# Near and global keys laid out behind each block's own, and attention in steps of eight heads

## The chip, the cores and the metric

One core of a Trainium2 chip runs the whole program. The metric is the device time of one execution in microseconds (us); lower is better. Engines are named as in the profile: PE is TensorE's matmul stream, PEld its weight loads, DVE is VectorE, ACT ScalarE, POOL GpSimd, SP SyncE, whose queue issues nearly all loads.

## The reference, cut to what matters

Attention over 4 batches, 8 heads, 768 positions of 64 features; then a feed-forward layer 512 to 2048 to 512 on 3072 tokens; then a mixture of eight experts with 384 tokens each.

```python
n_global, n_local = (8, 96)
...
is_global = pos[None, :] < int(n_global)
is_local = (rel >= 0) & (rel < int(n_local))
keep = is_global | is_local
dist = np.where(is_global & ~is_local, float(n_local), np.abs(rel).astype(np.float32))
...
scores = scores + bias[None, :, :, :]
scores = np.where(keep, scores, -1000000000.0)
...
a = a / (np.sum(a, axis=-1, keepdims=True) + 1e-09)
return np.matmul(a, v).astype(np.float32)
...
h = x @ w_in
g = h * (1.0 / (1.0 + np.exp(-h)))
return (g @ w_out).astype(np.float32)
```

A block of 128 queries needs its own 128 keys, the 95 keys in front of it and the 8 global ones: 103 keys beside its own.

## The kernel before

**Tiling.** Attention works on 24 blocks of 128 tokens (six per batch). A group is four heads of one block; there are 48 groups. For each group `scores` (L413) issues four matmuls of 64 rows by 256 columns in float32 (128 columns for the first block of a batch, which has nothing in front): two heads at a time lie on the two halves of the array's rows, and their scores go to two PSUM banks taken from the ring `TP` (banks 0, 1, 2). Then, per pair of heads, the softmax: a DVE operation that adds the table of distances and finds the maximum (L453), an exponential on ACT (L457), and on DVE the reciprocal of the sum (L461, L462) and the scaling (L464). `turn` (L468) transposes the probabilities of two pairs on PE (L478) and ACT copies each to SBUF (L482). `weigh` (L485) multiplies them with the values: eight matmuls of 128 columns (L500), into bank 5. After the second group of a block `features` (L505) splits the result in two parts for the feed-forward layer.

The 256 keys are those of the block and of the whole block before it. `keys` (L377) keeps two halves of one tile for each group of heads, the even and the odd block, and loads each block's keys once; from the third block of a batch on, POOL first copies the eight global keys into the half of the block in front (L387). `values` (L401) has three buffers and loads eight global rows into the older one (L408).

**The feed-forward layer** works on chunks of two blocks: sixteen items a chunk, each `item` (L538) being 12 matmuls of 256 columns (L552), a tanh and a few elementwise operations (L566 to L572), and `product` (L575) six matmuls of 512 columns (L587 to L589). The hidden values of items go to the ring `HB` (banks 3 and 4); the accumulators lie in banks 6 and 7.

**Order.** The program is written as slots (L739, L780). Where chunks 2 to 9 are worked on, a slot holds one item and its predecessor's product, and `a` counts the slots by heads: every fourth slot visits a group. In that visit PE does the values of the group four slots back and the scores of the new one as one task (from slot `PAIRED` = 56 on), and two slots later `turn`. A planner then orders all tasks: `Plan.order` (L188) simulates five engines with guessed durations, and of the tasks that are ready it starts the one with the lowest `pri` (by default the order in which they were written). The gate's dot products on DVE (L659) have 200 added to theirs, so they go last. Within an engine the order is then fixed.

Early on (slots up to 55, chunks 0 and 1) attention runs ahead of the feed-forward layer, whose weights are loaded as 8-byte numbers and converted by ACT, DVE and POOL (L354 to L372).

After the front part, `Back` routes tokens and runs the experts; it reuses the attention's buffers (L1512) for its small tables, and gathers and scatters rows with 48 indirect DMAs issued by POOL (L1311, L1430).

Of the kernel before, what the change touches and what calls it, by code (L numbers as in the profile page):

```python
# [225 lines left out]

def sub_ap(ap, offset, dims):
    return bass.AP(tensor=ap.tensor, offset=ap.offset + offset, ap=[list(d) for d in dims])
# [6 lines left out]
class Front:  # L235


    def __init__(self, tc, plan, room, banks, main, small, pages, qT, kT, vT, w_in, w_out, w_gate, n_global, n_local, x2d, L,
                 xd=None, dbg=None):
        self.tc, self.nc, self.p = tc, tc.nc, plan  # L240
        self.room, self.banks, self.main, self.small, self.pages = room, banks, main, small, pages
        self.qT, self.kT, self.vT = qT, kT, vT
# [24 lines left out]
    def consts(self):  # L267
# [4 lines left out]
        t = self.banks.take(6, lambda t: t.rearrange("p a b -> p (a b)"))  # L272
# [6 lines left out]
        p.add(PE, 0.427 * NWARM, warm, r=[one], w=[t])  # L279
# [3 lines left out]
        base = self.once("v20", [128, 4, 128], BF16, self.small)  # L283

        self.T = self.once("T", [128, H, 3, 128], BF16, self.small)
# [3 lines left out]
        def near():  # L289
# [4 lines left out]
            g.affine_select(T[:, 1], t, pattern=[[1, 128]], compare_op=ALU.is_ge, fill=MASK, base=nl - 1,  # L294
# [7 lines left out]
            if ng < 128:  # L302
                nc.vector.tensor_copy(T0[:, ng:], T[:, 1, ng:])

        def before():

            r, T = rel()[:, 0], base()
            g.iota(r, pattern=[[1, 128]], base=-128, channel_multiplier=-1, allow_small_or_imprecise_dtypes=True)
            g.affine_select(T[:, 0], r, pattern=[[1, 128]], compare_op=ALU.is_ge, fill=MASK, base=nl - 129,
                            channel_multiplier=-1)  # L310
            if ng:
                g.memset(T[:, 0, :ng], -float(nl))
            nc.vector.tensor_copy(T[:, 2], T[:, 0])
# [15 lines left out]
        for h in range(H):  # L329
            p.add(DVE, 0.2, lambda h=h: nc.vector.tensor_scalar(part[h](), base()[:, :3], 2.0 ** (2 - h), None, op0=ALU.mult),  # L330
# [46 lines left out]
    def keys(self, bl, e):  # L377

        nc, p, ng = self.nc, self.p, self.ng
        i, j = bl % NB, bl % 2  # L380
        if e not in self.K:
            t = self.once(f"k{e}", [128, 2, 2, 128], F32, self.small)
            self.K[e] = t, t.parts(*(lambda t, j=j: t[:, :, j] for j in range(2)))
        t, b = self.K[e]
# [4 lines left out]
        p.add(SP, 0.6, lambda: nc.sync.dma_start(b[j](), self.half_block(self.kT, bl, e)), w=[b[j]],  # L389
              pri=12 * e + 24 * bl - 99 if bl < DB else None)  # L390

    def half_block(self, t, bl, e):
        return sub_ap(t, bl * 128 * DM + 256 * e, [[DM, 128], [1, 256]]).rearrange("p (a s) -> p a s", a=2)
# [7 lines left out]
    def values(self, bl, e):  # L401
        nc, p, ng = self.nc, self.p, self.ng
        c = 4 * e * D
        rows = lambda n, bl: self.vT[bl * 128:bl * 128 + n, c:c + 4 * D].rearrange("s (h d) -> s h d", d=D)
        if bl % NB > 1 and ng:

            w = self.V[bl - 1, e]
            p.add(SP, 0.6, lambda: nc.sync.dma_start(w()[:ng], rows(ng, bl - bl % NB)), w=[w])  # L408
        v = self.V[bl, e] = self.once(f"v{bl % 3}{e}", [128, 4, D], F32, self.small)
        p.add(SP, 0.6, lambda: nc.sync.dma_start(v(), rows(128, bl)), w=[v], pri=12 * e + 24 * bl - 90 if bl < DB else None)  # L410


    def scores(self, u, before=None):  # L413

        nc, p = self.nc, self.p
        bl, h0 = divmod(u, H)
        i = bl % NB
        n = 1 if i == 0 else 2
        e = h0 // 4
        k, kb = self.K[e]  # L420
        q = self.qs[bl, e]
        s = [self.half("tp", 4) for _ in range(2)]

        def qk():
            for a in range(2):
                for j in range(2):
                    r = slice(64 * j, 64 * j + 64)
                    nc.tensor.matmul(s[j]()[:, n * a:n * a + n], q()[r, a], k()[r, a, :n], start=True, stop=True)  # L428

        if before:  # L430
            dur, av, r, w, then = before

            def both():
                av()
                qk()

            p.add(PE, dur + 0.43 * n, both, r=[*r, q, *kb[:n]], w=[*w, *s])
            then()
        else:
            p.add(PE, 0.43 * n, qk, r=[q, *kb[:n]], w=s)  # L440
        for a in range(2):
            z = self.ring("z", NZ, [128, 2, 2, 128], F32)
# [3 lines left out]
            for j in range(2):  # L446
# [3 lines left out]
                def soft1(a=a, j=j, h=h, nb=nb, zs=zs):  # L450
                    T = self.Th[h]()
                    t = self.T0h[h]()[:, None] if i == 0 else (T[:, 1:3] if i % 2 == 0 else T[:, 0:2])
                    nc.vector.tensor_tensor_reduce(zs[j]()[:, :n], s[j]()[:, n * a:n * a + n], t, -0.125, 3.0e38, ALU.add,  # L453
                                                   ALU.min, nb())

                p.add(DVE, t_dve(128 * n), soft1, r=[s[j], self.T0h[h] if i == 0 else self.Th[h]], w=[zs[j], nb])
                p.add(ACT, 0.1 + 0.2 * n, lambda j=j, nb=nb, zs=zs, ss=ss: nc.scalar.activation(  # L457
                    zs[j]()[:, :n], zs[j]()[:, :n], AF.Exp, bias=nb(), scale=-1.0, accum_out=ss[j]()),
                      r=[nb], w=[zs[j], ss[j]], lat=0.09)
            v = nc.vector  # L460
            p.add(DVE, 0.073, lambda r=r, sm=sm: v.tensor_scalar(r(), sm(), 1e-9, None, op0=ALU.add), r=[sm, *ss], w=[r])  # L461
            p.add(DVE, 0.1, lambda r=r: v.reciprocal(r(), r()), w=[r])  # L462
            for j in range(2):
                p.add(DVE, t_fast(128 * n), lambda j=j, zs=zs, r=r: v.tensor_scalar(  # L464
                    zs[j]()[:, :n], zs[j]()[:, :n], r()[:, j:j + 1], None, op0=ALU.mult), r=[r], w=[zs[j]])
            self.z[u + 2 * a] = zs

    def turn(self, u):  # L468
        nc, p = self.nc, self.p
        n = 1 if (u // H) % NB == 0 else 2  # L470
        for a in range(2):
# [13 lines left out]
    def weigh(self, u):  # L485
# [8 lines left out]
        vs = [self.V[bl - (bl + b) % 2, h0 // 4] for b in range(n)]  # L494
# [285 lines left out]
    def slot(self, a, items, ws):  # L780
# [13 lines left out]
        if near and a is not None and a % 4 == 0:  # L794
            w = self.weigh(a - 4) if unit(4) else None
            if w and not (unit(0) and a >= PAIRED):
                dur, av, r, o, then = w
                self.p.add(PE, dur, av, r=r, w=o)
                then()
                w = None  # L800
            if unit(0):
                self.scores(a, w)
        if near and unit(2) and a % 4 == 2:
# [745 lines left out]
```

## Time and profile before

| | us |
|---|---|
| median of 3 runs | 1089.94 |
| lowest, highest | 1089.39, 1091.43 |
| the profiled execution's own time | 1091.94 |
| its span, first to last instruction | 1090.2 |
| PE busy in the span | 1049.2 (96%) |
| DVE busy | 817.4 (75%) |
| ACT busy | 489.9 (45%) |
| POOL busy | 153.1 (14%) |

The profile is of one execution. Its span leaves out 1.7 us before the first and after the last instruction. A row of the timeline gives start, duration, engine, line, operation, and what is written and read; matmuls are pipelined, so the spacing of starts tells more than durations. "Idle before" is what the engine waited, and for whom. A row of the table by stretches gives the stretch, its length, the busy time and number of instructions of each engine, TensorE's granted clock as a share of full speed, and the DMA engines' share and rate.

### The profile page before, as it was taken

What the parts mean: (1) busy time and instruction counts of PE and PEld (TensorE: products, weight loads), DVE (VectorE), ACT (ScalarE), POOL (GpSimd) and SP (SyncE); (2) the same over time, 40 slices, a digit from 0 to 9 for tenths busy, and PEclk for the clock granted to TensorE, in tenths of its full rate; (3) what the DMA queues carried; (4) which work ended last, traced back from release to release, by engine and by line L of the source; (5) the groups of instructions that cost most, each with busy time, mean ns of one, the idle gap of its engine ahead of it and who ended that gap; (6) DMA issues with size and microseconds to landing.
All of it is one profiled execution on the core that took longest, in us unless ns stands there. A gap on an engine that the chain in (4) does not pass through costs nothing.

```text
span 1090.2 us, 20764 instructions
## 1 busy us (share of the span) xinstructions
PE 1049.2 (96%) x7541; PEld 893.0 (82%) x7541; DVE 817.4 (75%) x2734; ACT 489.9 (45%) x1243; POOL 153.1 (14%) x172
## 2 busy tenths in 40 slices
PE   7879989999999999999999999999999999999997
PEld 4657778888888888888888889976778888888996
DVE  7999768969596969787787866547878888984431
ACT  5766544454444444444444444413343443433431
POOL 2434541101000101000000000000011203211111
PEclk8989999999999999999999999999899999999999
DMA  5555532110111101120101100005336434524510
GB/s 176 159 159 158 170 107 69 31 49 21 45 45 29 36 30 51 31 64 21 45 17 50 31 26 2 1 20 174 108 107 213 132 119 175 174 93 162 176 64 29
DMA packets 71719, 91.79 MB, mean 84 GB/s; under 512 B 5312, under 2 KB 54720, under 8 KB 71616
## 3 DMA queue, kind: packets, MB, share of 16 engines
q1 hardware_dynamic: 67776, 77.87, 22.4%
q0 software_dynamic: 3840, 12.59, 3.4%
q8 instruction: 59, 0.97, 0.4%
q14 instruction: 44, 0.36, 0.1%
HBM read 77.86 MB, written 12.58 MB: 83 GB/s over the span
## 4 chain that ended last, share of the span: by engine, by line
PE 68%; issue 7%; DVE 7%; DMA 2%; POOL 1%; ACT 1%; POOLq 0%; SPq 0%; ACTq 0%; DVEq 0%
PE bank L552 20%; PE bank L1391 9%; PE bank L1417 8%; PE bank L587 7%; PE bank L588 6%; PE bank L589 6%; PE bank L500 3%; PE bank L428 3%; PE bank L478 2%; PE bank L1079 1%; PE bank L1332 1%; PE bank L682 1%; POOL out_dram L1430 1%; DMA st__9177<-in_moe_w_dram 1%; DMA out_dram<-wl__10561,v__8959 1%
## 5 line engine op out<-in xcount | busy, mean ns | idle before, releaser
L387 POOL TENSOR_SCALAR k__84<-k__84 128x16 f32<-128x16 f32 x16 | 4.6, 288 | 176.0 <-PE bank L428 108.7
L387 POOL TENSOR_SCALAR k__120<-k__120 128x16 f32<-128x16 f32 x16 | 4.1, 256 | 139.1 <-PE bank L428 78.7
L1079 PEld LDWEIGHTS <-z__8685 128*128 128x128 bf16 x280 | 9.6, 97 | 8.8 <-issue 3.6
L1311 POOL DMA_INDIRECT wl__9185<-x2d,v__8959 x1 | 1.3, 1336 | 97.9 <-DVE wh__9187 L1373 97.9
L1128 DVE TENSOR_SCALAR_CACHE_REDUCE v__8094<-bank 128x8 f32<-128x8 f32 (+1 forms) x28 | 4.4, 158 | 13.0 <-PE bank L1079 13.0
L634 DVE DVE_READ_ACCUMULATOR2_ANT L<- 128x1 f32 x160 | 12.9, 81 | 0.0
L1079 PEld LDWEIGHTS <-z__8695 128*128 128x128 bf16 x280 | 9.5, 96 | 1.5 <-issue 1.4
L1079 PEld LDWEIGHTS <-z__8690 128*128 128x128 bf16 x280 | 9.5, 96 | 0.0
L1321 PE MATMUL bank<-q__7831 128*128 128x512 bf16 x32 | 9.1, 439 | 0.0
L1372 ACT ACTIVATE wl__9009<-st__8966 128x512 fp32r<-128x512 f32 x1 | 0.6, 632 | 18.5 <-DMA st__8966<-in_moe_w_dram 18.5
L1321 PEld LDWEIGHTS <-q__7831 128*128 128x128 bf16 x32 | 3.1, 106 | 6.1 <-issue 3.9
L1069 DVE TENSOR_TENSOR z__8685<-v__8735,q__7831 128x1024 bf16<-128x1024 f16 (+1 forms) x14 | 7.8, 555 | 0.0
L1069 DVE TENSOR_TENSOR z__8690<-v__8735,q__7831 128x1024 bf16<-128x1024 f16 (+1 forms) x14 | 7.7, 550 | 0.0
L1069 DVE TENSOR_TENSOR z__8695<-v__8735,q__7831 128x1024 bf16<-128x1024 f16 (+1 forms) x14 | 7.7, 550 | 0.0
L1079 PE MATMUL bank<-v__8094,z__8685 128*128 128x8 bf16 x160 | 7.1, 168 | 0.0
L1131 PEld LDWEIGHTS <-q__7831 128*128 128x128 bf16 x28 | 2.7, 98 | 5.3 <-issue 5.0
L1079 PE MATMUL bank<-v__8094,z__8695 128*128 128x8 bf16 x160 | 6.9, 167 | 0.0
L1079 PE MATMUL bank<-v__8094,z__8690 128*128 128x8 bf16 x160 | 6.8, 166 | 0.0
L1430 POOL DMA_INDIRECT out_dram<-wl__11117,v__8959 x1 | 2.7, 2744 | 28.3 <-ACT wl__11117 L1429 28.3
L603 ACT ACTIVATE ax__8789<-bank 128x512 f32<-128x512 f32 x1 | 0.6, 598 | 12.8 <-PE bank L589 12.8
L277 PE MATMUL bank<-jk__77 128*128 128x512 bf16 x10 | 4.4, 631 | 1.5 <-DVE jk__77 L273 1.5
L1069 DVE TENSOR_TENSOR z__8685<-v__8735,q__7664 128x512 bf16<-128x512 f16 (+1 forms) x14 | 5.9, 419 | 0.0
(8066 smaller groups left out, 4579.9 us busy)
## 6 DMA issues: line engine op xcount, KB each, us to landing
k__84<-in_k_dram SPq DMA_DIRECT2D x24, 128.0 KB, 2.2
k__120<-in_k_dram SPq DMA_DIRECT2D x24, 128.0 KB, 2.2
st__189<-in_moe_w_in_dram SPq DMA_DIRECT2D x1, 512.0 KB, 3.9
st__230<-in_moe_w_out_dram SPq DMA_DIRECT2D x1, 512.0 KB
st__273<-in_moe_w_in_dram SPq DMA_DIRECT2D x1, 512.0 KB
st__346<-in_moe_w_out_dram SPq DMA_DIRECT2D x1, 512.0 KB
st__393<-in_moe_w_in_dram SPq DMA_DIRECT2D x1, 512.0 KB, 4.2
st__425<-in_moe_w_out_dram SPq DMA_DIRECT2D x1, 512.0 KB, 4.3
```

The lines of the kernel that those rows point to most:

```text
L428: nc.tensor.matmul(s[j]()[:, n * a:n * a + n], q()[r, a], k()[r, a, :n], start=True, stop=True)
L478: nc.tensor.transpose(pt()[:, n * j + b], zs[j]()[:, b], self.ident())
L500: nc.tensor.matmul(o()[64 * j:64 * j + 64, h0 // 2 + a], vs[b]()[:, 2 * a + j], ps[a]()[:, n * j + b], start=b == 0, stop=b == n - 1)
L552: nc.tensor.matmul(h(), w, x(d), start=k == 0, stop=k == 11)
L587: nc.tensor.matmul(a(), gh()[:, j], oh(), start=f == 0, stop=False)
L588: nc.tensor.matmul(a(), gh()[:, j], ol(), start=False, stop=False)
L589: nc.tensor.matmul(a(), gl()[:, j], oh(), start=False, stop=f == NF - 1)
L1069: self.p.add(DVE, t_fast(n * CPART), lambda s=s, c=c, sh=sh: v.tensor_tensor(c().rearrange("p b (j w) -> p b j w", w=2), key()[:, s, None, ...
L1079: nc.tensor.matmul(cnt(), cs[j](b), D()[:, i], start=i == 0, stop=i == NBLK - 1)
L1391: nc.tensor.matmul(h()[:, :RB], w()[:, d], x(), start=d == 0 and i == 0, stop=d == 3 and i == 2)
L1417: nc.tensor.matmul(a(), g()[:, j], w(), start=f == 0 and i == 0, stop=f == NF2 - 1 and i == 2)
L1430: p.add(POOL, 1.1, lambda: nc.gpsimd.indirect_dma_start(out=self.out[k * RB + j], out_offset=bass.IndirectOffsetOnAxis(ap=self.idx[k]()[:, ...
```

## The change

The host lays out, for each block and head pair, the block's own 128 keys and behind them `W2` = 104 others: 8 global, 95 near, 1 of padding. The values of these 104 come as a second tensor. So `scores` works on 232 columns instead of 256, the tables and the softmax too, `turn` transposes 128 and 104 columns, and `weigh` contracts over 128 and 104 rows. The copy of global keys on POOL and the small loads of global values go; key loads have two buffers per group of heads, and there is a load of far values beside the load of own values. From slot 56 to 183 attention goes in steps of eight heads: `visit` does, as one task on PE, the values of the two older groups and the scores of the two new ones, one of whose four banks is taken from the items' ring (`"h"`); the four pairs are turned two, three, five and six slots later. The second group's softmax has its `pri` raised by `LATE`, a second pair's by `STEP`. The buffers of turned probabilities go from three to four. The ring of POOL's DMA descriptors is halved.

```diff
+        ts = [self.banks.take(i, lambda t: t.rearrange("p a b -> p (a b)")) for i in (*TP0, HB[0])]
...
-                nc.tensor.matmul(t(), one()[:, :128], one(), start=True, stop=True)
+                nc.tensor.matmul(ts[i % len(ts)](), one()[:, :128], one(), start=True, stop=True)
...
-        if i > 1 and ng:
-
-            p.add(POOL, 0.174, lambda: nc.gpsimd.tensor_scalar(b[1 - j]()[:, :, :ng], b[j]()[:, :, :ng], 1.0, 1.0,
-                                                               ALU.mult, ALU.mult), r=[b[j]], w=[b[1 - j]])
...
+        t = self.K[bl, e] = self.once(f"k{e}{bl % 2}", [128, 2, 128 + self.W2], F32, self.small)
+        self.p.add(SP, 0.6, lambda: self.nc.sync.dma_start(t(), self.half_block(self.kT, bl, e)), w=[t],
+                   pri=12 * e + 24 * bl - 99 if bl < DB else None)
...
-            p.add(SP, 0.6, lambda: nc.sync.dma_start(w()[:ng], rows(ng, bl - bl % NB)), w=[w])
...
+        for x, src, n in (("v", self.vT, 128), ("vb", self.vB, self.W2))[:1 if bl % NB == 0 else 2]:
+            v = self.once(f"{x}{bl % 2}{e}", [128, 4, D], F32, self.small)
+            p.add(SP, 0.6, lambda v=v, src=src, n=n: nc.sync.dma_start(
+                v()[:n], src[bl * n:(bl + 1) * n, c:c + 4 * D].rearrange("s (h d) -> s h d", d=D)),
...
+    def visit(self, new, old):
+
+        done = [self.weigh(u) for u in old]
+
+        new = [self.scores(u, len(new) == 2 and i == 0, LATE * i) for i, u in enumerate(new)]
+        todo = [*done, *new]
+
+        def all():
+            for t in todo:
+                t[1]()
+
+        self.p.add(PE, sum(t[0] for t in todo), all, r=[b for t in todo for b in t[2]],
+                   w=list({id(b): b for t in todo for b in t[3]}.values()))
+        for t in todo:
+            t[4]()
...
+        s = [self.half("h" if more and j else "tp", 4) for j in range(2)]
...
+                    self.nc.tensor.matmul(flat(s[j])[:, 256 * a:256 * a + n], q()[r, a], k()[r, a, :n], start=True, stop=True)
...
+        first = len(p.tasks) + late
         for a in range(2):
-            z = self.ring("z", NZ, [128, 2, 2, 128], F32)
+            pri = first + (STEP * a if PAIRED <= u < ALONE else a)
+            z = self.ring("z", NZ, [128, 2, 256], F32)
...
-                        nc.tensor.transpose(pt()[:, n * j + b], zs[j]()[:, b], self.ident())
+                        w = (128, self.W2)[b]
+                        nc.tensor.transpose(pt()[:w, n * j + b], zs[j]()[:, 128 * b:128 * b + w], self.ident())
...
-                        nc.tensor.matmul(o()[64 * j:64 * j + 64, h0 // 2 + a], vs[b]()[:, 2 * a + j], ps[a]()[:, n * j + b],
+                        nc.tensor.matmul(o()[64 * j:64 * j + 64, h0 // 2 + a], vs[b]()[:rows[b], 2 * a + j], ps[a]()[:rows[b], n * j + b],
...
+            if PAIRED <= a < ALONE:
+                if r == 0:
+                    self.visit([a + 4, a], [a - 4] if a == PAIRED else [a - 8, a - 4])
+                if r in TURNS:
+                    self.turn(a - r + TURNS[r][0], [TURNS[r][1]])
...
-NZ, NP = 4, 3
-PAIRED = 56
+NZ, NP = 4, 4
+
+PAIRED, ALONE, LATE, STEP = 56, NU - H, 40, 20
+TURNS = {2: (4, 0), 3: (4, 1), 5: (0, 0), 6: (0, 1)}
...
-    nc = bacc.Bacc("TRN2", target_bir_lowering=False, num_devices=1, dynamic_dma_scratch_size=8192)
+    nc = bacc.Bacc("TRN2", target_bir_lowering=False, num_devices=1, dynamic_dma_scratch_size=4096)
```

## Rows read from the trace of the kernel before

**Rows 1.** Busy time, share of the span and instructions, whole run: TensorE.
```profile
PE 1049.2 (96%) x7541; PEld 893.0 (82%) x7541; DVE 817.4 (75%) x2734; ACT 489.9 (45%) x1243; POOL 153.1 (14%) x172
```

**Rows 2.** Busy time by stretches: two early ones, and the stage of chunks 2 to 9.
```profile
0.00:54.50 54.50, 44.45 (x270) 30.51 (x270) 47.01 (x166) 35.59 (x100) 18.10 (x31) 0.87 0.55 167
54.50:109.00 54.50, 45.16 (x294) 35.34 (x295) 49.65 (x121) 35.59 (x87) 23.68 (x22) 0.94 0.53 158
...
163.50:654.00 490.50, 488.44 (x3485) 423.02 (x3485) 396.15 (x1400) 227.40 (x657) 30.31 (x45) 1.00 0.12 38
```

**Rows 3.** Waits of PE between 163 and 654 us, longest first: line, releaser, us.
```profile
PE bank L478 <- DVE z__6587 L464: 0.8, 1, 0.8
```

**Rows 4.** Timeline of PE: a visit with 256 keys, one with 128.
```profile
452.66 0.39 PE L589 MATMUL bank<-wh__1348,gl__5473 128*128 128x512 f32 x1
452.98 0.44 PE L500 MATMUL bank<-ph__5458,v__4854 128*64 128x128 f32 x4
...
454.00 1.13 PE L428 MATMUL bank<-k__120,q__5011 64*128 64x256 f32 x8
455.06 0.50 PE L587 MATMUL bank<-wh__1460,gh__5499 128*128 128x512 f32 x1
455.40 0.39 PE L588 MATMUL bank<-wl__1469,gh__5499 128*128 128x512 f32 x1
...
511.75 0.44 PE L500 MATMUL bank<-ph__6162,v__5563 128*64 128x128 f32 x4
...
512.34 0.72 PE L428 MATMUL bank<-k__120,q__5723 64*128 64x128 f32 x8
512.98 0.38 PE L552 MATMUL bank<-xTh__5000,wh__1588 128*128 128x256 f32 x1
```

**Rows 5.** Scores, timeline of L428: slots 64 and 176, 28 groups apart.
```profile
L428 PE MATMUL bank<-k__84,q__1803 x8: 376/376/480, 211.1 to 211.9; 64*128 64x256 f32 x8
...
L428 PE MATMUL bank<-k__84,q__6961 x8: 376/376/480, 614.0 to 614.8; 64*128 64x256 f32 x8
```

**Rows 6.** Timeline of PE: one pair turned, and the matmul behind it.
```profile
447.80 0.60 PE L478 MATMUL bank<-ident__79,z__5375 128*128 128x128 f32 x4
448.15 0.48 PE L587 MATMUL bank<-wh__1219,gh__5422 128*128 128x512 f32 x1
```

**Rows 7.** Weight loads of scores (64 rows) and items (128 rows), ns min/median/max.
```profile
L428 PEld LDWEIGHTS bank<-k__84,q__4847 x8: 182/186/187, 440.9 to 441.5; 64*128 64x128 f32 x8
...
L552 PEld LDWEIGHTS bank<-xUh__4287,wh__1185 x4: 186/192/192, 442.0 to 443.1; 128*128 128x128 f32 x4
```

**Rows 8.** Timeline of DVE: softmax at 256 and at 128 columns, a gate dot.
```profile
443.55 0.41 DVE L453 CUSTOM_DVE_ANT_0 z__5375<-bank,T__141 128x256 f32<-128x256 f32 x1
...
443.89 0.42 DVE L453 CUSTOM_DVE_ANT_0 z__5393<-bank,T__141 128x256 f32<-128x256 f32 x1
...
446.32 0.61 DVE L464 TENSOR_SCALAR z__5375<-z__5375,r__5417 128x256 f32<-128x256 f32 x2
...
7.15 0.29 DVE L453 CUSTOM_DVE_ANT_0 z__159<-bank,T__122 128x128 f32<-128x128 f32 x1 [1.32 <-PE bank L428]
...
7.37 0.29 DVE L453 CUSTOM_DVE_ANT_0 z__159<-bank,T__122 128x128 f32<-128x128 f32 x1
...
8.80 0.48 DVE L464 TENSOR_SCALAR z__159<-z__159,r__181 128x128 f32<-128x128 f32 x2
...
440.52 0.69 DVE L659 CUSTOM_DVE_ANT_0 jk__5351<-xl__5235,st__1783 128x512 bf16<-128x512 f32 x1
```

**Rows 9.** Copies of global keys on POOL (L387) in the first stretch.
```profile
0.00:54.50 54.50, 1.87 (x6) 0.87 0.55 167
```

**Rows 10.** Timeline of the start: first load of keys, first scores.
```profile
0.80 0.44 SPq L389 DMA_DIRECT2D k__84<-in_k_dram  x1
...
5.89 1.23 PE L428 MATMUL bank<-k__84,q__113 64*128 64x128 f32 x8
```

**Rows 11.** Timeline of POOL: the last scatter, with POOL's idle time before.
```profile
1084.46 0.97 POOL L1430 DMA_INDIRECT out_dram<-wl__13194,v__8959  x1 [1.07 <-ACT wl__13194 L1429]
```

More of the change, by code (lines that the diff above doesn't have):

```diff
@@ L401, in values, with scores @@
     def values(self, bl, e):
-        nc, p, ng = self.nc, self.p, self.ng
+        nc, p = self.nc, self.p
         c = 4 * e * D
-        rows = lambda n, bl: self.vT[bl * 128:bl * 128 + n, c:c + 4 * D].rearrange("s (h d) -> s h d", d=D)
-        if bl % NB > 1 and ng:
-            w = self.V[bl - 1, e]
-            p.add(SP, 0.6, lambda: nc.sync.dma_start(w()[:ng], rows(ng, bl - bl % NB)), w=[w])
[L409 to L415, printed above, removed]
+        self.V[bl, e] = []
+        for x, src, n in (("v", self.vT, 128), ("vb", self.vB, self.W2))[:1 if bl % NB == 0 else 2]:
+            v = self.once(f"{x}{bl % 2}{e}", [128, 4, D], F32, self.small)
+            p.add(SP, 0.6, lambda v=v, src=src, n=n: nc.sync.dma_start(
+                v()[:n], src[bl * n:(bl + 1) * n, c:c + 4 * D].rearrange("s (h d) -> s h d", d=D)),
+                  w=[v], pri=12 * e + 24 * bl - 90 if bl < DB else None)
+            self.V[bl, e].append(v)
+    def visit(self, new, old):
[9 more added lines that the diff above has]
+            t[4]()
+    def scores(self, u, more=False, late=0):
         bl, h0 = divmod(u, H)
-        i = bl % NB
-        n = 1 if i == 0 else 2
         e = h0 // 4
-        k, kb = self.K[e]
-        q = self.qs[bl, e]
-        s = [self.half("tp", 4) for _ in range(2)]
+        n = 128 if bl % NB == 0 else 128 + self.W2
+        k, q = self.K[bl, e], self.qs[bl, e]
+        s = [self.half("h" if more and j else "tp", 4) for j in range(2)]
         def qk():
@@ L427, in qk, with softmax @@
                     r = slice(64 * j, 64 * j + 64)
[L428 to L440, printed above, removed]
+                    self.nc.tensor.matmul(flat(s[j])[:, 256 * a:256 * a + n], q()[r, a], k()[r, a, :n], start=True, stop=True)
+        return 0.43 * n / 128, qk, [q, k], s, lambda: self.softmax(u, s, late)
+    def softmax(self, u, s, late):
+        nc, p = self.nc, self.p
+        bl, h0 = divmod(u, H)
+        i = bl % NB
+        n = 128 if i == 0 else 128 + self.W2
+        first = len(p.tasks) + late
         for a in range(2):
-            z = self.ring("z", NZ, [128, 2, 2, 128], F32)
+            pri = first + (STEP * a if PAIRED <= u < ALONE else a)
+            z = self.ring("z", NZ, [128, 2, 256], F32)
             zs = z.parts(*(lambda t, j=j: t[:, j] for j in range(2)))
@@ L493, in weigh @@
         ps = [self.P.pop(u + 2 * a) for a in range(2)]
-        vs = [self.V[bl - (bl + b) % 2, h0 // 4] for b in range(n)]
+        vs = self.V[bl, h0 // 4]
+        rows = 128, self.W2
         def av():
@@ L792, in slot @@
             self.weights(u)
[L794 to L803, printed above, removed]
-            self.turn(a - 2)
+        if near and a is not None and a >= 0:
+            r = a % 8
+            if PAIRED <= a < ALONE:
[3 more added lines that the diff above has]
+                    self.turn(a - r + TURNS[r][0], [TURNS[r][1]])
+            else:
+                if r % 4 == 0:
+                    old = [u for u in ((a - 8, a - 4) if a == ALONE else (a - 4,)) if 0 <= u < NU]
+                    if a < PAIRED and old:
+                        self.visit([], old)
+                        old = []
+                    if old or unit(0):
+                        self.visit([a] if unit(0) else [], old)
+                if r % 4 == 2 and unit(2):
+                    self.turn(a - 2)
         for c, f in items:
@@ L1494, in attention_moe_kernel @@
         x2d = dp.tile([NTOK, DM], F32, name="x2d")
[L1496 removed]
+        near = is_near(n_global, n_local)
         xd = None
```

100 lines of the change are left out of this document (56 added, 44 removed).

## Prediction

> **What bounds the kernel now.** First the page's busy times: PE is busy for 96% of the span [rows 1]. That is an average, so next the busy times by stretches [rows 2]. From 163.5 to 654 us, where chunks 2 to 9 and most of attention run, PE is busy for 488.4 of 490.5 us at the full granted clock (1.00), while DVE has 396.2, ACT 227.4 and POOL 30.3. In the first 109 us it is otherwise: PE is busy for 44.5 and 45.2 of 54.5 us, DVE for 47.0 and 49.7. The view of waits says whether PE's busy time hides stalls: in the long stage its longest wait is 0.8 us, for a softmax's scaling [rows 3]. So in that stage only work that leaves PE counts, and early on work that leaves DVE counts most. What attention costs PE is read from the timeline. From the scores of slot 64 to those of slot 176 are 402.9 us, or 14.4 us for a group and its four items [rows 5].
>
> One visit [rows 4]: the last matmul of an item starts at 452.66, and the next of its kind would start 0.23 later (the usual spacing, 0.23 us); the values start at 452.98, 0.09 late. Values to scores is 1.02, scores to the next item 1.06, and that item's first matmul takes 0.34 to the second, 0.11 more than usual. Together 2.28 us. A visit in a block with nothing in front has half the values and half the columns: 0.59 and 0.64 [rows 4]. The differences, 0.43 and 0.42, are the price of the work itself; so 0.16 us (1.02 less twice 0.43) and 0.22 us (1.06 less twice 0.42) are spent whatever the amount. With 0.09 and 0.11 a visit has **0.58 us of fixed cost** and 1.70 us of work.
>
> **The change, part by part.**
>
> *Two visits become one.* From slot 56 to slot 184 there are 33 visits before and 17 after (56, 64 and so on to 184), each with all values first and all scores behind. 16 visits go. If the second group's matmuls follow the first's without a break, each takes its 0.58 us along: 16 x 0.58 = 9.3 us. If the part of the scores is paid for each group anyway, 0.36 is left and 5.8 us. I take 9.3: inside one visit four pairs of matmuls already follow each other at the price of the work, and a second group is more of the same.
>
> *232 columns for 256 in the scores.* 0.42 us for 128 columns [rows 4] is 3.3 ns a column, 79 ns a group for 24 columns. From slot 56 on there are 34 groups, four of them in first blocks of a batch: 30 x 0.079 = 2.4 us, all on PE. The bounds are nothing (if weight loads, 186 ns [rows 7], keep the spacing up) and 2.4; I take 2.4.
>
> *Values over 104 rows, turns of 104 columns.* The values' matmuls stream 128 columns of probabilities as before, over fewer rows. The rows show no price for rows: a weight load with 64 rows takes 186 ns, one with 128 rows 186 to 192 [rows 7]. The Trainium skill says the same of the loads in "TensorE: Matmul & The Clock Gate", section "LDWEIGHTS (loading the stationary operand)": their time goes with the columns and not with the contraction dimension. By that rule, which speaks against much of what this change cuts, this part is worth nothing; priced by rows of keys it would be what the second rival below has. I take nothing for the values. A turn of a pair is 0.35 us from its start to the next item's [rows 6]; half of it has 104 columns of weights instead of 128, but the same 128 columns stream, so I take nothing here and keep 30 x 2 x 0.35 x 0.5 x 24/128 = 2.0 us as the upper bound. There are four turns for eight heads before and after.
>
> *Softmax.* The maximum takes 0.34 us at 256 columns and 0.22 at 128, start to start [rows 8]: 0.9 ns a column; two scalings 0.61 and 0.48, 1 ns a column of both. A group (four maxima, two pairs of scalings) saves 24 x (4 x 0.9 + 2 x 1.0) = 0.13 us on DVE. In the long stage PE covers it (DVE has 94 us free there [rows 2]); if that cover goes it would be 30 x 0.13 = 4 us. Early there are ten groups with 256 keys: 1.3 us, which counts where DVE is the bound.
>
> *Copies of global keys.* Six copies, 1.87 us of POOL in the first 54.5 us [rows 9], and with them the wait of a key load for the copy, behind which SP's weight loads stand. I take 0.7 us for that. So the early stage gives 2 us. It is also where the order may shift: bounds -3 and +5 us, a few of the 20 us for which PE idles there [rows 2].
>
> *Loads.* By their shapes, the keys of a group go from 128 to 232 KB, and 40 loads of 104 KB stand where 32 loads of 8 KB stood: 8.9 MB more, some 2.5 MB of it before 163 us, and eight more issues on SP at about 0.44 us [rows 10]. The DMA engines are 0.55 and 0.53 busy early and 0.12 later [rows 2], so this goes beside other work. A key load now has two buffers and waits only for the scores two blocks back. The first load is issued at 0.80 and the first scores start at 5.89, behind the warm-up matmuls [rows 10]; a load nearly twice as long fits in that. If the cover went, 2.5 MB at 160 GB/s [rows 2] would be 16 us; that is a rival.
>
> *What waits.* The one PE task for eight heads waits for four turned pairs and four banks at once, and the next item's matmuls stand behind it on PE. The last pair is turned two slots ahead (5.6 us); its copy on ACT is ready long before. The scores of slot a+4 come four slots earlier, with their whole softmax; the older group's values come four slots later, which is what the fourth buffer is for. The items' ring lends a bank: below.
>
> *The end.* A smaller descriptor ring could make POOL wait. Its last scatter came after 1.07 us of idle time [rows 11] and POOL is busy for 14% [rows 1]; nothing, upper bound about 1 us on the last scatter.
>
> Sum: 9.3 + 2.4 + 2 = 13.7 us. The profiled execution took 1091.94 us; 1078.2 after. It is 2.0 us above the median of 1089.94, so the median forecast is 1076.2, say **1076 us**. What is late next is still PE, in the same stage.
>
> **The rivals.**
>
> *The fixed cost stays with the group* (chance 0.12). If the 0.58 us belong to each group's change of shapes rather than to the visit, only columns and the early stage pay: 2.4 + 2 = 4.4 us, 1085.5. For it: values and scores each have their own share. Against it: within a visit nothing is paid between pairs.
>
> *Everything shrinks by the keys* (0.07). If values and turns also cost by keys, a group saves another 0.43 x 24/128 + 0.066 = 0.15 us, 30 times 4.4 us: 1071.6. Against it stand the weight loads [rows 7].
>
> *The borrowed bank stalls PE: slower* (0.07). Each eight-head visit takes one of the items' two banks, so the second item behind it cannot start until DVE has read four sets of scores from that visit. PE has the other scores (about 0.8), an item and a product (14.4 - 2.28 - 0.86, over four, is 2.8) to do meanwhile: 3.7 us. DVE needs 4 x 0.34 = 1.4 us and may have a feature split and an item's two operations in front (1024 columns at 0.9 ns and three times some 0.1 us of start, as the maxima [rows 8] have it: 1.3 us), as well as gate dots of 0.69 us [rows 8]. With one dot it holds by 0.3 us. It decides when the stall passes 13.7 / 16 = 0.86 us a step, that is from two more dots in front; then it is 1.1 us, 17.6 in all, 3.9 us slower: 1093.8. Against it: dots have the lowest priority. The Trainium skill, in "TensorEngine Tiling (Array Packing)", section "Gotcha 1: PSUM Pressure", warns of this side of row tiling: different row tiles write to different banks, so eight heads side by side ask for four. By that rule alone the time would be this rival's; the kernel before takes two banks a visit and hardly waits [rows 3], so no row here shows the case of four.
>
> *The early loads give it back: no change* (0.05). If the larger loads were not hidden, up to 16 us early against 13.7: about 1090.
>
> **How the numbers follow.** The forecast has 0.69. Its own bounds: 5.8 to 9.3 for the visits, 0 to 2.4 for columns, 0 to 2 for turns, -3 to +5 early; taken together mostly 8 to 17 us, 1073 to 1082. The range goes on to the second rival and over the first, 1070 to 1086, and leaves out the other two and some of the early stage. About 0.2% (2.2 us) is what a measurement can tell from no change. Faster by more: 0.69 + 0.12 + 0.07 = 0.88; slower: 0.06 of the 0.07; the rest, 0.06, within.
>
> **What would show it.** In the changed profile a full visit should last 2 x 1.70 + 0.58 - 0.16 = 3.8 us where two took 4.6; eight heads with eight items 28.0 us instead of 28.8; PE without waits in the stage; the copies gone. It is wrong if PE waits in that stage for DVE in front of an item, if a visit lasts over 4.3 us, or if the stage begins later than before by more than 3 us.

## The result, and the profile after

The changed kernel takes 1081.49 us (median of 6 runs, 1078.96 to 1084.85), the kernel before, run beside it, 1090.12. The ratio is 0.9913 with an interval of 0.9891 to 0.9935: 9.5 us less (7.1 to 11.9); the two medians themselves are 8.6 us apart. The forecast was 1076, with a range of 1070 to 1086; it was on the right side, 5.5 us too low. One run of the kernel before, of 1659 us, lies far above its other five and is left out of the ratio. The profiled execution took 1079.03 us, with a span of 1077.3.

The page's line of busy times of the changed kernel answers to [rows 1]:

```profile
PE 1033.2 (96%) x7541; PEld 893.0 (83%) x7541; DVE 809.1 (75%) x2733; ACT 487.0 (45%) x1243; POOL 143.8 (13%) x141
```

TensorE has as many instructions as before and is busy for 16 us less, at the same 96%. POOL has 31 instructions fewer: the copies are gone. To see where the time went, both kernels are cut at the same two events: the store of chunk 1's result and that of chunk 9's (SP, L604 before and L619 after). In the view by windows, columns are span, then busy time of PE, PE's weight loads, DVE, ACT, POOL, the granted clock, and the DMA's share and GB/s. The kernel before:

```profile
0.00:184.00 184.00, 159.35 (x1012) 123.26 (x1013) 150.71 (x430) 110.36 (x290) 72.42 (x79) 0.94 0.47 145
184.00:641.97 457.97, 456.20 (x3255) 395.16 (x3255) 368.47 (x1306) 211.53 (x615) 26.85 (x40) 1.00 0.12 37
641.97:1090.20 448.23, 433.60 (x3279) 374.59 (x3279) 298.23 (x999) 167.98 (x340) 53.80 (x53) 0.98 0.33 108
```

The changed kernel:

```profile
0.00:175.63 175.63, 151.74 (x990) 119.62 (x990) 146.78 (x412) 106.44 (x280) 68.77 (x71) 0.94 0.54 170
175.63:627.22 451.59, 447.52 (x3259) 397.88 (x3260) 364.44 (x1323) 212.92 (x625) 21.04 (x17) 1.00 0.16 50
627.22:1077.30 450.08, 433.97 (x3295) 375.55 (x3295) 297.85 (x999) 167.67 (x340) 53.97 (x53) 0.99 0.33 107
```

So 8.4 us went early, 6.4 in the long stage, and 1.9 came back behind it. The long stage is the reliable part: in three profiles of the changed kernel it took 451.6, 451.7 and 451.6 us, in three of the kernel before 458.0 each time. The early part is not: the store of chunk 1 came at 175.6, 177.5 and 177.8 after, and at 184.0, 178.7 and 181.7 before. The experts' part, from the first gather to the last scatter, took 323.2 to 329.3 us in the four profiles with the old attention and 323.8 to 330.9 in the ten with the new; a cost of some 2 us there can't be told from this spread. The counts also say that work changed sides. Before the first cut the changed kernel has 22 fewer TensorE instructions: among them, by line, 8 of scores (a group), 4 of turns (a pair) and 8 of values. At their prices (0.95, 0.35 and 0.44) that is, by estimate, 1.7 us of work that it does later.

A full visit of eight heads, in the timeline of PE of the changed kernel, answers to [rows 4]:

```profile
427.85 0.28 PE L567 MATMUL bank<-xUh__4339,wl__1164 128*128 128x256 f32 x1
428.06 0.44 PE L515 MATMUL bank<-ph__5263,v__4709 128*64 128x128 f32 x4
428.33 0.39 PE L515 MATMUL bank<-ph__5263,vb__4714 104*64 104x128 f32 x4
428.55 0.39 PE L515 MATMUL bank<-ph__5322,v__4709 128*64 128x128 f32 x4
428.77 0.39 PE L515 MATMUL bank<-ph__5322,vb__4714 104*64 104x128 f32 x4
...
429.65 0.39 PE L515 MATMUL bank<-ph__5213,vb__4742 104*64 104x128 f32 x4
429.97 1.05 PE L444 MATMUL bank<-k__4795,q__5068 64*128 64x232 f32 x8
430.86 0.95 PE L444 MATMUL bank<-k__4765,q__4772 64*128 64x232 f32 x8
431.74 0.50 PE L602 MATMUL bank<-wh__1091,gh__5356 128*128 128x512 f32 x1
432.08 0.40 PE L603 MATMUL bank<-wl__1103,gh__5356 128*128 128x512 f32 x1
```

Counted as in the prediction (the usual spacing of items, 0.12 or 0.23 us, taken off at either end) it lasts 3.88 us; 3.8 was forecast, and two visits of before took 4.56. Behind the first, the values' rows follow each other at 0.22 us whether they are of 128 or of 104 keys, and the scores are 0.89 and 0.88 apart. Eight heads with eight items take 28.2 us (394.5 us from the scores of slot 64 to those of slot 176, 14 steps), where 28.0 was forecast and 28.8 stood. The turn answers to [rows 6], 0.36 us to the next item where 0.35 stood:

```profile
448.23 0.60 PE L492 MATMUL bank<-ident__79,z__5446 128*128 128x128 f32 x4
448.59 0.36 PE L567 MATMUL bank<-xUh__4339,wh__1781 128*128 128x256 f32 x1
```

What was not forecast stands in the view of waits of PE over the long stage (releaser; us in all, times, longest), which answers to [rows 3]:

```profile
PE bank L602 <- ACT gh__4640 L585: 1.0, 1, 1.0
PE bank L604 <- DVE gl__7460 L587: 0.8, 1, 0.8
PE bank L604 <- DVE gl__6046 L587: 0.8, 1, 0.8
PE bank L604 <- DVE gl__3198 L587: 0.8, 1, 0.8
PE bank L567 <- DVE nb__2597 L466: 0.3, 1, 0.3
PE bank L567 <- DVE nb__6865 L466: 0.2, 1, 0.2
PE bank L567 <- DVE nb__4740 L466: 0.2, 1, 0.2
```

PE idles for 4.1 us in this stage (451.59 less 447.52), 1.8 before. The last three waits are for the borrowed bank, 0.7 us in all. The first four have another cause, one every 112 us or so. The timeline of DVE ahead of the wait for gl__3198:

```profile
254.08 0.69 DVE L649 CUSTOM_DVE_ANT_0 jk__3168<-ax__2896,xh__2121 128x512 bf16<-128x512 f32 x1
...
255.03 1.73 DVE L674 CUSTOM_DVE_ANT_0 jk__3180<-ax__3113,st__1885 128x512 bf16<-128x512 f32 x1
...
256.69 0.41 DVE L587 TENSOR_TENSOR gl__3198<-t__3166,gh__3182 128x256 fp32r<-128x256 f32 x1
```

POOL's timeline and PE's at the same time:

```profile
254.92 1.29 POOL L661 TENSOR_TENSOR ax__3174<-wh__753,wl__771 128x512 f32<-128x512 f32 x1 [5.83 <-DVE L L649]
```

```profile
257.16 0.50 PE L604 MATMUL bank<-wh__1038,gl__3198 128*128 128x512 f32 x1 [0.78 <-DVE gl__3198 L587]
```

A dot of the gate usually takes 0.69 us. This one takes 1.73: POOL began to add two halves of a weight 0.11 us ahead of it, and until about half a microsecond after POOL's end the dot is not done. The operation that TensorE needs is next on DVE. Twelve dots of the stage last 1.72 to 1.78 us. Whether the addition is the cause is what gatesum, below, asks.

### The profile page after: what moved, and what is told of

Its sections match the earlier page's. It is cut to its first block, busy times and chain, and to the rows that moved or that the text cites. A ratio compares the mean times of both kernels' runs of the same rounds, so it can differ in the third digit from the quotient of the medians.

```text
span 1077.3 us, 20712 instructions
## 1 busy us (share of the span) xinstructions
PE 1033.2 (96%) x7541; PEld 893.0 (83%) x7541; DVE 809.1 (75%) x2733; ACT 487.0 (45%) x1243; POOL 143.8 (13%) x141
## 3 DMA queue, kind: packets, MB, share of 16 engines
q1 hardware_dynamic: 65800, 86.99, 25.3%
## 4 chain that ended last, share of the span: by engine, by line
PE 65%; DVE 13%; issue 10%; DMA 3%; POOL 2%; ACT 1%; POOLq 0%; DVEq 0%; ACTq 0%; SPq 0%
PE bank L567 19%; PE bank L1414 8%; PE bank L1440 8%; PE bank L602 6%; PE bank L604 6%; PE bank L603 6%; PE bank L515 3%; PE bank L492 2%; PE bank L444 2%; PE bank L1102 1%; PE bank L1355 1%; DMA xh__10127<-in_moe_w_dram 1%; PE bank L697 1%; DMA out_dram<-wl__10623,vb__9021 1%; DMA st__9223<-in_moe_w_dram 1%
## 5 line engine op out<-in xcount | busy, mean ns | idle before, releaser
L1344 PE MATMUL bank<-q__7895 128*128 128x512 bf16 x32 | 8.8, 429 | 0.0
L661 POOL TENSOR_TENSOR xl__5294<-wh__1211,wl__1232 128x512 f32<-128x512 f32 x1 | 1.3, 1294 | 53.8 <-DVE L L649 53.8
L661 POOL TENSOR_TENSOR xl__3880<-wh__845,wl__855 128x512 f32<-128x512 f32 x1 | 1.3, 1296 | 53.7 <-DVE L L649 53.7
L661 POOL TENSOR_TENSOR xl__6712<-wh__1609,wl__1627 128x512 f32<-128x512 f32 x1 | 1.3, 1283 | 52.3 <-DVE L L649 52.3
L661 POOL TENSOR_TENSOR ax__5961<-wh__1423,wl__1432 128x512 f32<-128x512 f32 x1 | 1.3, 1298 | 49.2 <-DVE L L649 49.2
L661 POOL TENSOR_TENSOR ax__7375<-wh__1805,wl__1815 128x512 f32<-128x512 f32 x1 | 1.3, 1297 | 48.5 <-DVE L L649 48.5
L661 POOL TENSOR_TENSOR ax__4529<-wh__1038,wl__1043 128x512 f32<-128x512 f32 x1 | 1.4, 1359 | 47.1 <-DVE L L649 47.1
L661 POOL TENSOR_TENSOR ax__3113<-wh__589,wl__599 128x512 f32<-128x512 f32 x1 | 1.3, 1297 | 46.8 <-DVE L L649 46.8
L1102 PE MATMUL bank<-v__8156,z__8747 128*128 128x8 bf16 x160 | 7.1, 168 | 0.0
L1102 PE MATMUL bank<-v__8156,z__8757 128*128 128x8 bf16 x160 | 6.9, 166 | 0.0
```

Of the source, the lines that this page charges most:

```text
L1102: nc.tensor.matmul(cnt(), cs[j](b), D()[:, i], start=i == 0, stop=i == NBLK - 1)
```

## The experiments

All kernels here compute the whole reference. Each ratio is to the kernel before on the same chip; its median was 1096.29 in the first group (again to w128), 1090.68 in the second (before2 to before_ring) and 1094.34 in the third. "Stage" is the time between the two cuts.

**The changed kernel again** (again; no edit).

> The changed kernel itself, as the base of this group. Its six timed runs lay at 1079 (three) and 1083 to 1085 us (three), with 1090 for the kernel before beside both. If the spread is a matter of the chip, this one lies at one of the two levels with all its runs, 6 to 11 us below the kernel before; if of the single execution, its runs mix both.

Ratio 0.991 (0.9877 to 0.9942), span 1080.4, stage 451.7. The gain is repeatable. Its four runs lie 5.4 us apart on one chip (1082.05 to 1087.48), so the spread of the first six is one of single executions, at least in part.

**Values and scores in turn** (interleaved). The same visit of eight heads, but values, scores, values, scores in place of all values and then all scores.

```
-        todo = [*done, *new]
+        todo = [t for pair in zip(done, new) for t in pair] if len(done) == len(new) == 2 else [*done, *new]
```

> Same work, but inside a full visit of eight heads the order is values, scores, values, scores instead of values, values, scores, scores. If the fixed cost belongs to the change of shapes (0.16 us from values to scores and 0.22 us from scores on, some 0.4 to 0.6 us more per visit), the 15 full visits lose it again: 6 to 9 us slower than the changed kernel, and a full visit takes 4.3 to 4.5 us. If it belongs to entering a PE task from an item (waits, semaphores), nothing changes: within 1 us.

Ratio 0.995 (0.993 to 0.9971), stage 455.9. Its timeline of PE:

```profile
431.00 0.28 PE L567 MATMUL bank<-xUh__4339,wl__1164 128*128 128x256 f32 x1
431.21 0.44 PE L515 MATMUL bank<-ph__5263,v__4709 128*64 128x128 f32 x4
...
432.24 1.05 PE L444 MATMUL bank<-k__4787,q__5068 64*128 64x232 f32 x8
433.23 0.44 PE L515 MATMUL bank<-ph__5144,v__4730 128*64 128x128 f32 x4
...
434.26 1.05 PE L444 MATMUL bank<-k__4766,q__4774 64*128 64x232 f32 x8
435.24 0.50 PE L602 MATMUL bank<-wh__1091,gh__5356 128*128 128x512 f32 x1
435.58 0.40 PE L603 MATMUL bank<-wl__1103,gh__5356 128*128 128x512 f32 x1
```

The visit takes 4.23 us, 0.35 more. With the same matmuls in it, that is the price of changing between values and scores twice more. Fifteen such visits lie in the stage: 5.3 us; the stage is 4.3 longer and the median 4.9, both less than the 6 to 9 that were expected. The order inside the visit, not the size of the visit alone, carries most of the gain.

**Four heads at a step, with the new keys** (fourheads): the change without its merging.

```
-PAIRED, ALONE, LATE, STEP = 56, NU - H, 40, 20
+PAIRED, ALONE, LATE, STEP = 56, 56, 40, 20
-                    old = [u for u in ((a - 8, a - 4) if a == ALONE else (a - 4,)) if 0 <= u < NU]
+                    old = [u for u in (a - 4,) if 0 <= u < NU]
```

> Near keys only, but four heads at a step as before (values and scores of one group each, every four slots). If the merged visits are what the step of eight heads brings, 16 visits pay 0.58 us again: about 9 us slower than the changed kernel, less what PE waits for in the eight-head stage (some 2 us): 6 to 9. If the fixed cost stays with the group, equal within 1 us.

Ratio 0.9974 (0.9956 to 0.9992). Its timeline of PE and its windows:

```profile
435.18 0.44 PE L515 MATMUL bank<-ph__5340,v__4698 128*64 128x128 f32 x4
...
436.21 1.05 PE L444 MATMUL bank<-k__4722,q__4879 64*128 64x232 f32 x8
437.19 0.38 PE L567 MATMUL bank<-xUh__4331,wh__1268 128*128 128x256 f32 x1
```

```profile
177.74:636.08 458.34, 456.05 (x3255) 394.55 (x3255) 366.09 (x1306) 208.46 (x615) 21.58 (x17) 1.00 0.16 49
```

A visit takes 2.20 us, where the kernel before has 2.28 [rows 4]: the columns are saved as forecast, 0.08 us a group, for the 27 groups with 232 columns in the stage. The median is 7.4 us above again's, within the 6 to 9 that were expected. Yet the stage is 458.3 where it was 458.0 in the kernel before. The 2.2 us went into small waits, between the six matmuls of a product and around the turns; what makes them in this order was not tried. Two visits of 2.20 less one of 3.88 is 0.52 us: what a merging is worth.

**256 columns again** (w128): 24 columns of padding more, in eight-head steps.

```
-    n = max(n + n % 2, 2)
+    n = 128
```

> Eight heads at a step, but 128 far keys a block (25 of them masked) instead of 104, so scores and softmax have 256 columns, and values and turns 128 rows and columns. If only scores and softmax cost by columns: 2.4 us in the long stage and about 1.3 us early, 3 to 4 us slower than the changed kernel. If values and turns cost by keys too: 0.15 us a group more, about 8 us slower.

Ratio 0.9951 (0.9929 to 0.9974), stage 455.4. Its timeline of PE:

```profile
437.82 0.39 PE L515 MATMUL bank<-ph__5192,v__4721 128*64 128x128 f32 x4
438.04 0.39 PE L515 MATMUL bank<-ph__5192,vb__4729 128*64 128x128 f32 x4
438.36 1.14 PE L444 MATMUL bank<-k__4775,q__5067 64*128 64x256 f32 x8
439.33 1.03 PE L444 MATMUL bank<-k__4743,q__4755 64*128 64x256 f32 x8
440.29 0.38 PE L567 MATMUL bank<-xUh__4339,wh__1251 128*128 128x256 f32 x1
```

Scores are 0.97 and 0.96 us apart for 0.89 and 0.88: again 0.08 a group, the 0.079 of the prediction. The values of 128 keys follow each other at 0.22 like those of 104. "TensorE: Matmul & The Clock Gate" of the Trainium skill, section "LDWEIGHTS (loading the stationary operand)", which has the load's time independent of the contraction dimension, agrees with that 0.22. The stage is 3.8 us longer, more than the 2.2 of the columns; the rest is in waits and longer spacings.

**Both kernels once more** (before2, after2; no edit), for the spread of the early part.

> The kernel before itself, for its trace on the chip of this group. Stores of chunk 1 at about 184 us, from there to the store of chunk 9 458 us, from the first gather to the last scatter 319 us. If a chip shifts these, this run says by how much.

> The changed kernel itself on the same chip: store of chunk 1 some 6 to 8 us earlier than the kernel before, the stretch to the store of chunk 9 6 us shorter. From the first gather to the last scatter: if the change costs the experts' part nothing, within 1 us of the kernel before on this chip; if it does (descriptor ring, other places of small buffers), 2 to 4 us longer.

1087.35 and 1079.76 us, one run each: stages of 458.0 and 451.6; chunk 1 stored at 178.7 and 177.8, 0.9 us apart, where the first pair of profiles had 8.4 and 6 to 8 were expected. The experts' part took 323.6 and 323.8 us, so in this pair the change costs it nothing.

**One key buffer for each group of heads** (onebuf).

```
-        t = self.K[bl, e] = self.once(f"k{e}{bl % 2}", [128, 2, 128 + self.W2], F32, self.small)
+        t = self.K[bl, e] = self.once(f"k{e}0", [128, 2, 128 + self.W2], F32, self.small)
-            (f"k{i}{j}", 2 * front.K2) for i in range(2) for j in range(2)] + [
+            (f"k{i}0", 2 * front.K2) for i in range(2)] + [
```

> The changed kernel with one buffer of keys per group of heads, so that a key load waits for the scores of the block in front, as it did before, and what stands behind it on SP's queue waits too. If that wait was what the early stage gained from, the store of chunk 1 comes 3 to 6 us later and the run is as much slower; if the early gain is DVE's shorter softmax or the order, within 1 us.

Ratio 0.9938 (0.9915 to 0.9962), stage 451.7, chunk 1 at 180.0, 2.2 us behind after2 on the same chip. SP now waits for scores ahead of its key loads, and by that shift the second buffer has a use; but a shift of this size lies within what one kernel shows from run to run, and the intervals of the two kernels overlap. Not settled.

**The smaller descriptor ring, in the kernel before** (before_ring).

```
-    nc = bacc.Bacc("TRN2", target_bir_lowering=False, num_devices=1, dynamic_dma_scratch_size=8192)
+    nc = bacc.Bacc("TRN2", target_bir_lowering=False, num_devices=1, dynamic_dma_scratch_size=4096)
```

> The kernel before with the descriptor ring halved, nothing else. If POOL's 48 indirect DMAs have room enough: no change, within 1 us. If the ring is why the experts' part takes 2 to 4 us longer in the changed kernel's traces: that much slower.

Ratio 0.9987 (0.9971 to 1.0002); the experts' part took 324.1 us, 323.6 with the larger ring. No cost.

**The gate's sums on DVE** (gatesum, in the changed kernel; gatesum_before, in the kernel before). The same edit in both:

```
-        p.add(POOL, 1.225, lambda: nc.gpsimd.tensor_tensor(s(), oh().bitcast(F32), ol().bitcast(F32), ALU.add),
+        p.add(DVE, 0.602, lambda: nc.vector.tensor_tensor(s(), oh().bitcast(F32), ol().bitcast(F32), ALU.add),
```

> The changed kernel with the twelve or so sums of the gate's two weight halves (128x512, POOL, 1.29 to 1.36 us each) made on DVE instead. Theory A (the sum on POOL holds up the gate dot that DVE runs at the same moment, 1.73 us in place of 0.69, and TensorE then waits for the gelu's operation queued behind that dot): no dot of the gate over 0.8 us is left, the four TensorE waits of 0.8 to 1.0 us on gl and gh go, and the stretch from the store of chunk 1 to that of chunk 9 falls from 451.6 to about 448.5 us. Theory B (those waits come from DVE having too much queued in the paired visits, and the long dot is only where it shows): DVE has one operation of about 0.7 us more for each sum, the waits stay or grow, and the stretch is 451.5 to 453 us. Either way the total moves by 3 us at most.

> The same edit in the kernel before, where the same long dots stand but TensorE waits for 1.8 us in the whole stretch. Theory A: the stretch stays at 458.0 us, within 0.7, since there is nothing to win. Theory B expects the same or up to 1 us more. If the stretch falls by 2 us or more here too, the collision is a cost of both kernels and no part of what the change lost.

The changed kernel with it takes 1077.18 us, ratio 0.9831 (0.9808 to 0.9854), better than both kernels; its stage is 6.3 us shorter, twice what theory A had (451.6 to about 448.5). In all it is 8.6 us below copies, the run on the same chip that is nearest to the changed kernel, where 3 at most were expected; where the 2.3 us beyond the stage lie was not found. Its windows:

```profile
180.80:626.10 445.30, 445.18 (x3259) 398.59 (x3258) 361.97 (x1339) 215.06 (x626) 0.24 (x1) 1.00 0.17 51
```

And its timeline of DVE, where a sum now stands between two dots:

```profile
259.41 0.69 DVE L674 CUSTOM_DVE_ANT_0 jk__3196<-ax__3130,st__1885 128x512 bf16<-128x512 f32 x1
...
260.02 0.69 DVE L661 TENSOR_TENSOR ax__3198<-wh__753,wl__771 128x512 f32<-128x512 f32 x1
260.63 0.69 DVE L674 CUSTOM_DVE_ANT_0 jk__3205<-ax__3130,st__1885 128x512 bf16<-128x512 f32 x1
```

PE idles for 0.12 us of the stage, and the view of its waits is empty. DVE does 16 operations more than in the changed kernel and is busy for 2.5 us less (361.97 for 364.44). The kernel before with the same edit has a ratio of 0.9953 (0.9931 to 0.9974):

```profile
180.50:634.60 454.10, 454.10 (x3254) 395.35 (x3255) 366.35 (x1323) 212.57 (x615) 5.05 (x24) 1.00 0.12 37
```

Its stage falls too, by 3.9 us, which neither theory had forecast. So the collision is a cost of both kernels, and only 2.4 us of the 6.3 are the change's own loss.

It is not the dots alone that are held up. In the kernel before, two scalings of a softmax took 2.73 us, 0.61 as a rule [rows 8], while POOL made two sums:

```profile
543.99 2.73 DVE L464 TENSOR_SCALAR z__6587<-z__6587,r__6626 128x256 f32<-128x256 f32 x2
```

```profile
544.02 1.29 POOL L646 TENSOR_TENSOR xl__6636<-wh__1539,wl__1554 128x512 f32<-128x512 f32 x1 [2.59 <-DVE r__6634 L461]
545.26 1.32 POOL L646 TENSOR_TENSOR xl__6636<-wh__1640,wl__1664 128x512 f32<-128x512 f32 x1
```

The wait for this z__6587 is the longest of the kernel before [rows 3]: a sign of the collision stood in the rows from the start. Nor does the changed kernel pay more because more is held up. In its stage 13 DVE operations, the twelve dots and one of the gelu, last over 0.25 us longer than is usual for their line and shape, 13.3 us in all. In the kernel before there are 15 (eight dots, six scalings, one of the gelu), 14.9 us; with the sums on DVE there is none in either. The difference is in what TensorE loses by each. Set the start of every matmul beside that of the same matmul in the run with the sums on DVE: the changed kernel falls behind in steps. Behind the four dots ahead of its first four waits they are 1.06, 1.71, 1.07 and 1.06 us, behind the others 1.4 in all. In the kernel before they are 0.43, 1.01, 0.48, 1.53 (the two scalings above) and 0.43, and nothing behind the other nine operations. Between the steps the distance stays within 0.03 us, but for short stretches in which the two orders differ; so the gain goes with the collisions and not with some other effect of the edit on the order. Why a step is larger in one order than in the other was not tried.

Without the collision the change takes 8.8 us off the stage (454.1 to 445.3), and the two medians, 1089.35 and 1077.18 us, are 12.2 apart.

**The copies of global keys put back** (copies), in the changed kernel, behind the key load.

```
+        if bl % NB > 1:
+            g = lambda: t()[:, :, 128:128 + self.ng]
+            self.p.add(POOL, 0.174, lambda: self.nc.gpsimd.tensor_scalar(g(), g(), 1.0, 1.0, ALU.mult, ALU.mult), w=[t])
```

> The changed kernel with a copy of the global keys on POOL behind the key loads of the blocks from the third on, as the kernel before had for its four-block key tiles. If the removed copies and the waits on them are part of the early gain: the store of chunk 1 moves from about 177 to 178.5 us or later. If the early gain comes from fewer columns and visits alone: 177, within the spread of 2 us. The stretch from chunk 1 to chunk 9 stays at 451.6 in both, since each copy has a whole visit's time to be made in.

Ratio 0.9906 (0.9882 to 0.9931), as without them; stage 451.7. Chunk 1 was stored at 180.6, later than the 178.5 that were to speak for the copies, but gatesum's, without them, at 180.8 on the same chip. The copies cost nothing that shows. The run puts back POOL's work (each copy is of the columns onto themselves) and the wait of the scores for it, not the wait of a key load for the copy, 6.7 us over four early loads of the kernel before.

**No priorities for the second group's softmax** (noprio).

```
-PAIRED, ALONE, LATE, STEP = 56, NU - H, 40, 20
+PAIRED, ALONE, LATE, STEP = 56, NU - H, 0, 1
```

> The changed kernel with the second group's softmax of a paired visit no longer put back in the order (offsets 40 and 20 replaced by 0 and 1). If the softmax of two groups at once competes with the gelu's operations on DVE: waits of TensorE on gl, t and nb in the long stretch grow from 4 us in all to 6 or more, and the stretch is 453.5 us or longer. If DVE's reserve swallows the burst whatever its order: 451.6 us, within 0.5.

Ratio 0.9937 (0.9912 to 0.9962). Its windows, and the longest of its waits of PE in the stage:

```profile
178.40:635.40 457.00, 452.20 (x3258) 397.97 (x3258) 364.33 (x1323) 214.16 (x625) 21.32 (x17) 1.00 0.16 50
```

```profile
PE bank L602 <- ACT gh__4642 L585: 1.1, 1, 1.1
PE bank L604 <- DVE gl__3184 L587: 0.4, 1, 0.4
```

The stage is 5.4 us longer and most of the 6.4 us that the change had won there is gone, with the same work. DVE is busy for 364.3 of 457.0 us. Its spare time does not help, because, by the releasers named, what TensorE waits for is the gelu's operations, which now stand behind the second group's softmax in DVE's and ACT's order. Idle time is only 0.7 us of the 5.4 (4.8 in the stage, where 6 or more had been expected); PE's busy time rises by 4.7, since a matmul that starts late after another one, but before the modelled end of that one, shows as longer spacing and not as idle time.

## Why the prediction was right, and where its sizes were off

**Visits become one: the mechanism right, the size a little high.** The forecast was 0.58 us for each visit that goes. A merging gave 0.52 (2 x 2.20 less 3.88), 16 of them 8.3 us instead of 9.3. The first rival, that the fixed cost stays with the group, fell; but interleaved shows that 0.35 of the 0.52 is the change of shapes and stays if the visit keeps its old order inside.

**Columns: right on TensorE.** 0.08 us a group in fourheads and in w128, as forecast (0.079): 30 groups, 2.4 us. That it reaches the time is another matter: in fourheads none of it did, in that order.

**Values and turns: right at nothing.** 104 and 128 keys both take 0.22 us, a turn 0.36 for 0.35. The second rival, that all shrinks by keys, fell.

**"In the long stage PE covers it" and the paragraph on what waits: the step that failed.** With 16 x 0.52 and 2.4, 10.7 us should have gone between the first cut and the end of the front part. The stage gave 6.4. The rest of the front part, to the last store of a chunk, took 113.4 us where it was 112.9, and 1.7 us of work had come over from the early part: 6.4 - 0.5 + 1.7 = 7.6. With the gate's sums off POOL the same reckoning gives 8.8 - 0.5 + 1.7 = 10.0. So of the missing 3.1 us the collision of POOL's sums with DVE's operations took 2.4, and 0.7 is not placed. The prediction listed waits for dots of 0.69 us and did not see that some last 1.78: in the kernel before they stand too beside scalings that are held up, and cost 3.9 us. It took the view of waits to say whether busy time hides stalls [rows 3]; that view shows 1.8 us of idle time and its longest wait was a collision. Of its own signs the visit (3.88 for 3.8) and the eight heads (28.2 for 28.0) held; "PE without waits" did not (4.1 us idle), and three times PE waited for DVE in front of an item, which was to show it wrong. DVE's 94 us of free time were the wrong thing to look at. The cover is an order, as noprio shows: take the priorities away, and 5.4 us are lost.

**The borrowed bank: rightly a rival.** Its waits come to 0.7 us in all, and with the gate's sums moved none is left. The step that runs out of cover is the gelu's, not the bank's.

**The early part: 2 us forecast, about 1.6 measured, with little certainty.** The early code of the kernel before was profiled four times (with before_ring, and with gatesum_before, whose edit acts later), that of the changed kernel four times (with gatesum): chunk 1 at 184.0, 178.7, 181.7 and 180.5, mean 181.2, and at 175.6, 177.5, 177.8 and 180.8, mean 177.9. That is 3.3 us less, of which 1.7 is work put off. Two more kernels, interleaved and noprio, have the same order of instructions up to there, and chunk 1 at 176.6 and 178.4. One kernel's own values lie 5 us apart, so that chunk 1 comes sooner is likely, but the 1.6 us that are left lie within what such means can differ by; the 0.7 us for the copies were not seen, as far as copies and onebuf can show it. That 1.6 comes near to 2 is as much luck as reckoning.

**Loads: right.** The large queue moved 86.99 MB instead of 77.87, 9.1 more (the 8.9 of the forecast are in KB of 1024 bytes, which is the same); the DMA engines' share rose from 0.47 to 0.54 early and from 0.12 to 0.16 in the stage, and nothing shows a wait for it.

```profile
q1 hardware_dynamic: 65800, 86.99, 25.3%
```

**The end: right at nothing**, by before_ring and by before2 and after2, as far as the spread of the experts' part lets one see.

The sum as measured (the experts' part and the tail left out): 7.6 for the front part behind the first cut and about 1.6 early make 9.2, beside 9.5 (7.1 to 11.9) by the ratio. The forecast of 13.7 was too high by the visits' size (1.0), the collision (2.4) and smaller remainders.

## What to carry to other kernels

Where one engine is busy for all of a stage, look for the fixed cost of switching between kinds of work on it, and merge visits so that equal work stands together; smaller operands paid here only by the columns that stream, not by the rows. Look then at the order of the engine behind it and not at its free time: an operation that the bound engine needs must not stand behind a burst, nor behind one that another engine can hold up. A single operation at 2.5 times its usual length in a timeline is worth a look at what every other engine did in that moment; here it led to a larger gain than most of the change's own parts.

## What the hardware showed that was not expected

- An addition of two 128x512 tensors on POOL (1.29 us) held up a dot product of two such tensors on DVE from 0.69 to 1.73 us. Two scalings of 128x256 took 2.73 us beside two such additions, 0.61 as a rule. Moved to DVE the addition takes 0.69 us, and DVE's busy time in the stage falls. The Trainium skill describes it in "SBUF — State Buffer", section "🔬 SBUF: two separate sides": a DVE operation with two inputs in SBUF and a GpSimd operation that reads SBUF need the same pair of ports, the first has it for its whole length and the other is blocked. The trace agrees: the dot that began 0.11 us after POOL's addition ended 0.55 us after POOL's end, where a dot by itself takes 0.69.
- The view of waits shows less than a stall costs: for the kernel before it had 1.8 us of idle time in the stage, and 3.9 us went when the collision did.
- Changing between values (128 rows of keys on 64 columns) and scores (64 rows on 128) costs TensorE 0.35 us for one pair of changes, at a granted clock of 1.00.
- The same kernel's early part differs by 5 us between profiles, and its experts' part by 3 us (323.8 to 326.9 in three of the changed kernel), while its long stage repeats within 0.1 us. What makes the difference was not found.
